# Block-sparse attention with a two-layer network behind it: attention steps placed 0.08 units later in a hand-written order, from the fourth chunk on

## The chip, the cores and the metric

The kernel runs on one core of one Trainium2 chip. Five engines work side by side, each through its own list of instructions in order: TensorE (PE, with its weight loads PEld), VectorE (DVE), ScalarE (ACT), GpSimd (POOL) and SyncE (SP), which issues nearly all DMAs. They wait for one another through semaphores. The metric is device time in microseconds (us), a median over several runs.

## The reference

The kernel computes masked attention, and then a two-layer network over the attention's output. Cut to what matters:

```python
def _attn_ref(q, k, v, sampled_blocks):          # 4 batches, 8 heads, 768 positions, 64 wide
    scores = scale * np.matmul(q, k.transpose(0, 1, 3, 2))
    # a block of 32 queries sees: its neighbours, blocks 0 and 23, three sampled blocks;
    # the queries of blocks 0 and 23 see all keys
    scores = np.where(mask, scores, -1000000000.0)
    scores = scores - np.max(scores, axis=-1, keepdims=True)
    attn = np.exp(scores)
    attn = attn / (np.sum(attn, axis=-1, keepdims=True) + 1e-09)
    return np.matmul(attn, v)
def _moe_ref(x, w_in, w_out):                    # 3072 tokens, 512 wide, 2048 in the middle
    h = x @ w_in
    g = h - np.tanh(h)
    return g @ w_out
```

## The kernel before

The 3072 tokens go through the network in six chunks of 512, each made of four blocks of 32 queries of all four batches (`CHUNKS`). A chunk is worked off in 16 **units**, one for each 128 columns of the hidden layer, so that the program has 96 units. A unit u is:

- `first(u, c)`, c from 0 to 3: three products of 128x512 each, 12 in all, into the bank `hb[u % 2]` (bank 4 or 5 of PSUM). Weights and data are split into a high and a low part, which makes three products of one.
- `bent(u, ...)`: the function h - tanh(h), on ScalarE (`w`, `t`, `qq`, `mk`, `gh`), VectorE (`th`, `p1`, `p2`, `p3`, `cp`) and GpSimd (`gl`). `cp` is VectorE's predicated copy into the tile `t`; it is the last to read the bank of h.
- `second(u, j)`, j from 0 to 3: three products of 128x512 each (called a triple below), added into the banks 0 to 3. They run two units later than the unit's `first`.

When a chunk ends, `store` brings the four banks out, some two units later, on ScalarE and VectorE.

Attention is cut into **steps** (`Unit`, A0 to A55 below). A step of one block or of a part of an edge block is: `scores` (32 small products, 64 rows by 32 columns of the array, into the banks 6 and 7), `most` (VectorE, two maxima), `exps` (ScalarE, j = 1 and then j = 0), `turn` (8 transposes on TensorE, back into the banks 6 and 7), `copy` (one half on VectorE, one on ScalarE), `accum` (64 small products, 128 rows by 32 columns of the array) and `norm` (VectorE), then `put` on ScalarE and GpSimd into the operand of the chunk that comes next. For the two edge blocks three steps make one result, and `weigh` and `join` bring them together on VectorE. `accum` writes its result into bank 4 or 5, which is also a bank of h: it waits for the `cp` that last read this bank, and the next `first` into it waits for `norm`.

The order on every engine is the order of the program, and that is written by hand: every piece of work is put into a list with a due time in units (`at(time, f, ...)`), the list is sorted by time, and the engines run their instructions in that order. The attention that makes chunk m runs beside the network of an earlier one, in steps at the due times of `SLOTS`:

```python
SLOTS = [[0.17, 1, 2, 3, 4, 5], [22 + i for i in range(8)]] + [[16 * m + i * 16 // 11 for i in range(11)] for m in range(2, 5)]
    self.t = dict(s=t(0), m=t(0.08), e1=t(0.2), e0=t(0.3), turn=t(turn), c0=t(turn + 0.06), c1=t(turn + 0.05), pv=t(prod), norm=t(prod + 0.1))
```

The steps of chunks 3 to 5 (the fourth chunk on) are A24 to A55, in units 32 to 78. `scores` of a step is due 0.55 into its unit, and `accum` of the step before it 0.52 into the same unit. Where the next step lies one unit on, `turn` is due 0.66 after `scores` (`QUICK`); where it lies two units on, 1.0 after it (`TURN`). The network's own due times stay as they are: `second(u, j)` at u + 2.5 + 0.125 j, so that in every unit the four triples are due at 0.5, 0.625, 0.75 and 0.875; `first(u, c)` at u + 0.125 c; `p3` at u + 1.27 and `cp` at u + 1.49. The `join` pieces of the first two edge blocks are put where `quiet` finds the largest distance from due times of attention.

All instructions show as line L78 in the profile, since one helper issues them; they are told apart by engine, operation and tile.

Of the kernel before, what the change touches and what calls it, by code (L numbers as in the profile page):

```python
# [32 lines left out]
NU = NTOK // P // CT * NFT  # L33

LEAD, T0, RATE = 10, 10.25, 0.62
QUICK, TURN = 0.66, 1.0
NQ = 4
KEPT = 3
VW = H * (D + 1) // 2
# [27 lines left out]
class InOrder:  # L67


    class Engine:  # L70
        def __init__(self, tc, engine):
            self.tc, self.engine = tc, engine
# [44 lines left out]
class Unit:  # L117
# [27 lines left out]
    def at(self, half, j):  # L145

        return (half, self.b) if self.b else (self.f, (NB - 1) * half)


class Attention:  # L150
    def __init__(self, tc, k, q, v, samp, rows, ffn, ident, banks, att, sm, f2, rv, at):
        self.tc, self.nc = tc, InOrder(tc)
        self.k, self.q, self.v, self.ffn, self.ident, self.banks = k, q, v, ffn, ident, banks
        self.sm, self.f2, self.att, self.rv = sm, f2, att, rv
        self.ks = att.tile([P, 2, H, S], F32, name="ks")
        self.vws, self.krs, self.loans = {}, {}, {}
        ffn.lent = self.lent
        self.kx, self.vx = (att.tile([1, 66], I32, name=f"{n}x") for n in "kv")
        self.held = {}
        self.vals, self.qs, self.ve = {}, {}, {}  # L160
        self.ms, self.nbs, self.ps, self.pts, self.nbe, self.es, self.wts = ({} for _ in range(7))
        self.kept = [ffn.spare.bitcast(F32)[:, 256 * i : 256 * i + 256] for i in range(3)]

        units = []
        last = {}

        def add(c, time, **kw):
            u = Unit(len(units), c, time, **kw)
            u.i, u.before = c, last.get(c)
            if u.n < LEAD - 2:  # L170
                u.i, u.before = u.n % 2, units[u.n - 2] if u.n > 1 else None
            elif u.n < LEAD:
                u.before = units[u.n - 2]
            if u.b:
                last[c] = u
            units.append(u)

        for c in range(2):
            for b in CHUNKS[0]:
                add(c, 0, b=b)  # L180
        for c in range(2):
            add(c, 0, b=CHUNKS[1][0])
        for m, blocks in list(enumerate(CHUNKS))[1:]:
            steps = [(c, dict(b=b)) for b in blocks if 0 < b < NB - 1 for c in range(2)]
            edges = [(g // 2, dict(f=g % 2, k=k)) for g in EDGES.get(m, ()) for k in range(3)]
            steps += edges
            for i, (c, kw) in enumerate(steps[2 * (m == 1) :]):
                slots = SLOTS[m - 1]
                following = slots[i + 1] if i + 1 < len(slots) else 16 * m if m > 2 else slots[i] + 1
                add(c, slots[i] + 0.55, prod=following + 0.52, **kw)  # L190
        lead = lambda x: (x - T0) * RATE
        for u in units[:2]:
            at(lead(-9.05), self.load_q, u)
        for bt in range(2):
            at(lead(-9), self.load_k, 0, bt)
        at(lead(-9.1), self.load_samples, samp, rows)
        for bt in range(2):
            at(lead(-8.9), self.load_k, 1, bt)
        for u in units:
            t, n = u.t, u.n  # L200
            if u.b:
                if n > 1:
                    at(max(t["s"] - 2.0, units[n - NQ].t["s"] + 0.01) if n >= NQ else lead(-8.95 + 0.01 * n), self.load_q, u)
                at(max(t["s"] - 1.2, u.before.t["s"] + 0.01 if u.before else lead(-3)), self.gather_k, u)
                at(max(t["s"] - 2.0, u.before.t["pv"] + 0.01) if u.before else lead(-3 + 0.1 * n), self.gather_v, u)
            else:
                if u.k == 0:
                    at(units[n - 1].t["s"] + 0.02, self.load_q, u)
                at(units[n - 2].t["pv"] + 0.02, self.load_ve, u)
            at(t["s"], self.scores, u)  # L210
            at(t["m"], self.most, u)
            at(t["e1"], self.exps, u, 1)
            at(t["e0"], self.exps, u, 0)
            at(t["turn"], self.turn, u)
            at(t["c1"], self.copy, u, 1)
            at(t["c0"], self.copy, u, 0)
            at(t["pv"], self.accum, u)
            at(t["norm"], self.norm, u)
            if u.b:
                for x in "hl":  # L220
                    at(t["norm"] + (0.1 if x == "h" else 0.15), self.put, u, x)
            elif u.k == 2:
                at(t["e0"] + 0.12, self.weigh, u)
                end = 2 * u.c + u.f in EDGES[len(CHUNKS) - 1]
                quiet = iter([t["norm"] + 0.1 + 0.08 * j for j in range(6)] if end else self.quiet(units[u.n + 1 :], t["norm"]))
                for k in range(3):
                    for s in range(1 + k):
                        at(next(quiet), self.join, u, k, s)
                for i in range(2):
                    for x in "hl":  # L230
                        at(t["norm"] + 0.65 + 0.2 * i if end else LATE + 0.5 * (2 * u.c + u.f) + 0.25 * i, self.put, u, x, i)
# [489 lines left out]
```

## Time and profile before

| | before |
|---|---|
| time, median of 3 runs | 786.54 us (785.02 to 787.48) |
| the profiled execution's own time | 785.86 us |
| its span, first to last instruction | 784.1 us |
| TensorE busy | 728.9 us, 93% of the span |
| VectorE busy | 549.9 us, 70% |
| ScalarE busy | 479.2 us, 61% |
| GpSimd busy | 337.2 us, 43% |
| TensorE's mean granted clock over the span | 0.98 |

Shares of busy time are means over stages with different limits. The first 330 us or so hold the conversion of the weights and the attention of the first three chunks; the change touches what runs after about 312 us of the span, and up to about 675 us. Names in the rows: `ps` is any bank of PSUM, `kr` and `ks` are gathered and whole keys, `vw` and `ve` values, `pt` the transposed exponentials, `wo` and `wro` the second layer's weights, `t` the tile that `cp` completes. A product whose second operand is `gh` or `gl` is of `second`, one from `x` of `first`, one from `q` of `scores`, one from `pt` of `accum`, one from `ident` of `turn`.

### The profile page before, as it was taken

How to read it: one execution, taken by the hardware profiler on the slowest of the kernel's cores; microseconds unless marked ns; L12 is line 12 of the kernel's file. 1: busy time of each engine (PE TensorE's matmuls, PEld its weight loads, DVE VectorE, ACT ScalarE, POOL GpSimd, SP SyncE). 2: the span in 40 equal slices, each digit the busy share in tenths (PEclk: the TensorE clock that was granted, in tenths of full speed). 3: DMA queues.
4: the chain of work that ended last, by engine and by line, in shares of the span. 5: the costliest groups of instructions: out<-in, count | busy, mean ns of one | idle time of the engine just before them, and what ended most of it. 6: DMA issues, size and time to landing. Idle time of an engine off the chain costs nothing.

```text
span 784.1 us, 20699 instructions
## 1 busy us (share of the span) xinstructions
PE 728.9 (93%) x8128; PEld 564.7 (72%) x8128; DVE 549.9 (70%) x970; ACT 479.2 (61%) x1021; POOL 337.2 (43%) x406
## 2 busy tenths in 40 slices
PE   1777887999999999999999999999999998999996
PEld 0555555878777777777777777777877776788884
DVE  4566777779875765777676678676777675875653
ACT  1576756577767766565665666665666555554553
POOL 3685764667687646244322434321432211221211
PEclk9899999999999999999999999999999999999998
DMA  8887674489685686275746166565157364246542
GB/s 347 268 268 239 201 224 161 164 320 363 228 262 171 193 275 205 79 233 175 280 149 205 37 200 230 185 228 184 69 158 265 127 217 163 82 135 219 187 158 80
DMA packets 54260, 155.49 MB, mean 198 GB/s; under 512 B 9107, under 2 KB 15764, under 8 KB 53652
## 3 DMA queue, kind: packets, MB, share of 16 engines
q1 hardware_dynamic: 53780, 153.65, 58.6%
q8 instruction: 64, 1.05, 0.5%
q10 hardware_dynamic: 384, 0.52, 0.2%
q14 instruction: 32, 0.26, 0.1%
HBM read 133.17 MB, written 20.97 MB: 197 GB/s over the span
## 4 chain that ended last, share of the span: by engine, by line
PE 71%; DVE 7%; ACT 3%; issue 2%; POOL 1%; DMA 0%; DVEq 0%; POOLq 0%
PE ps L78 71%; DVE ps L78 3%; DVE t L78 1%; POOL gl L78 1%; DVE m L78 0%; ACT p L78 0%; ACT t L78 0%; DVE e L78 0%; ACT hs L78 0%; ACT wo L78 0%; ACT u L78 0%; DVE ob L78 0%; DVE cvti L78 0%; DVE cvto L78 0%; ACT gh L78 0%
## 5 line engine op out<-in xcount | busy, mean ns | idle before, releaser
L78 PE MATMUL ps<-x,wi 128*128 128x512 f32 x888 | 221.2, 393 | 0.0
L78 POOL TENSOR_TENSOR gl<-t,gh 128x512 fp32r<-128x512 f32 x96 | 124.3, 1295 | 215.3 <-ACT gh L78 69.5
L78 PE MATMUL ps<-wo,gh 128*128 128x512 f32 x592 | 192.2, 407 | 0.0
L78 PEld LDWEIGHTS ps<-x,wi 128*128 128x128 f32 x888 | 164.9, 188 | 35.5
L78 PEld LDWEIGHTS ps<-wo,gh 128*128 128x128 f32 x592 | 108.6, 190 | 36.9 <-issue 15.0
L78 ACT ACTIVATE u<-ps 128x512 f32<-128x512 f32 x96 | 57.3, 597 | 108.2 <-PE ps L78 108.2
L78 PE MATMUL ps<-wo,gl 128*128 128x512 f32 x296 | 117.6, 399 | 0.7 <-POOL gl L78 0.7
L78 POOL TENSOR_TENSOR x<-xt,x 128x256 fp32r<-128x256 f32 (+1 forms) x48 | 34.3, 715 | 161.8 <-ACT x L78 158.3
L78 POOL COPY kr<-ks 128x256 f32 (+2 forms) x188 | 98.5, 617 | 11.9 <-DMA ks<-k 11.7
L78 DVE TENSOR_REDUCE m<-ps 128x2 f32<-128x512 f32 x112 | 70.9, 673 | 19.1 <-PE ps L78 17.2
L78 DVE COPY_PREDICATED t<-mk,ps 128x512 f32<-128x512 int32 x96 | 71.8, 748 | 10.1 <-DVE ps L78 0.9
L78 DVE TENSOR_TENSOR ps<-ps,u 128x512 f32<-128x512 f32 x96 | 66.5, 692 | 13.7 <-ACT t L78 13.7
L78 ACT ACTIVATE p<-ps,nb 128x256 f32<-128x256 f32 x176 | 73.8, 471 | 2.9
L78 DVE SCALAR_TENSOR_TENSOR ps<-qq,ps 128x512 f32<-128x512 f32 x96 | 66.4, 692 | 12.9 <-ACT qq L78 8.6
L78 PEld LDWEIGHTS ps<-vw,pt 128*32 128x32 f32 x2816 | 44.4, 113 | 38.6 <-DVE t L78 10.1
L78 PE MATMUL ps<-vw,pt 128*32 128x65 f32 x2816 | 52.5, 227 | 20.4 <-DMA vw<-v 9.3
L78 ACT ACTIVATE qq<-u,bias 128x512 f32<-128x512 f32 x96 | 69.3, 722 | 0.0
L78 ACT ACTIVATE mk<-u,bias 128x512 f32<-128x512 f32 x96 | 69.1, 720 | 0.0
L78 DVE SCALAR_TENSOR_TENSOR ps<-u,ps 128x512 f32<-128x512 f32 x96 | 66.6, 693 | 2.5
L78 DVE TENSOR_TENSOR t<-t,ps 128x512 f32<-128x512 f32 x64 | 43.5, 680 | 35.2 <-ACT t L78 35.1
L78 PE MATMUL ps<-ident,p 128*128 128x128 f32 x448 | 62.4, 283 | 5.6 <-ACT p L78 4.2
L78 PEld LDWEIGHTS ps<-wo,gl 128*128 128x128 f32 x296 | 56.1, 189 | 15.4 <-POOL gl L78 1.9
(98 smaller groups left out, 980.2 us busy)
## 6 DMA issues: line engine op xcount, KB each, us to landing
wi<-w2i SPq DMA_DIRECT2D x65, 512.0 KB, 4.7
wo<-w2o SPq DMA_DIRECT2D x65, 512.0 KB, 3.7
vw<-v SPq DMA_DIRECT2D x186, 130.0 KB, 2.9
q<-q SPq DMA_DIRECT2D x52, 128.0 KB, 4.3
ve<-v SPq DMA_DIRECT2D x24, 260.0 KB, 4.0
ks<-k SPq DMA_DIRECT2D x4, 1536.0 KB, 8.4
rawo<-w SPq DMA_DIRECT2D x12, 512.0 KB, 4.3
rawi<-w SPq DMA_DIRECT2D x10, 512.0 KB, 4.7
```

The source lines that it names most:

```text
L78: r = f(*args, **kw)
```

## The change

One number is added, `SHIFT` = 0.08, to both due times of every step of chunks 3 to 5; all other times of a step are counted from these two.

```diff
-QUICK, TURN = 0.66, 1.0
+QUICK, TURN, SHIFT = 0.66, 1.0, 0.08
...
-                add(c, slots[i] + 0.55, prod=following + 0.52, **kw)
+                add(c, slots[i] + 0.55 + SHIFT * (m > 2), prod=following + 0.52 + SHIFT * (m > 2), **kw)
```

No instruction is added or taken away; the rows of each engine change places. Three places show how.

TensorE, unit 39: the end of `second(37, 0)` (bank `ps0`), `accum` of A28 (64 products into `ps4`, of which the first four and the last four are shown), `scores` of A29 (32 products into `ps6` and `ps7`) and `second(37, 1)` (bank `ps1`). Before:

```order
L78 MATMUL ps0_72<-wo37_5030,gh_37_5080 128x512 x2
L78 MATMUL ps0_72<-wo37_5030,gl_37_5089 128x512
L78 MATMUL ps4_76<-vw00_16_2920,pt28_1_5068 32x65 x4
...
L78 MATMUL ps4_76<-vw01_16_2921,pt28_0_5070 32x65 x4
L78 MATMUL ps6_78<-kr1_17_3090,q29_15_4982 32x256
...
L78 MATMUL ps7_79<-kr1_17_3090,q29_15_4982 32x256
L78 MATMUL ps1_73<-wo37_5030,gh_37_5080 128x512 x2
L78 MATMUL ps1_73<-wo37_5030,gl_37_5089 128x512
```

Now:

```order
L78 MATMUL ps0_72<-wo37_5030,gh_37_5080 128x512 x2
L78 MATMUL ps0_72<-wo37_5030,gl_37_5089 128x512
L78 MATMUL ps4_76<-vw00_16_2920,pt28_1_5073 32x65 x4
...
L78 MATMUL ps4_76<-vw01_16_2921,pt28_0_5075 32x65 x4
L78 MATMUL ps1_73<-wo37_5030,gh_37_5080 128x512 x2
L78 MATMUL ps1_73<-wo37_5030,gl_37_5089 128x512
L78 MATMUL ps6_78<-kr1_17_3090,q29_15_4987 32x256
...
L78 MATMUL ps7_79<-kr1_17_3090,q29_15_4987 32x256
L78 MATMUL ps2_74<-wo37_5030,gh_37_5080 128x512 x2
```

The triple for bank `ps1` now stands between `accum` and `scores`. This is so in all 31 places where an `accum` was followed at once by a `scores` (A24 with A25 up to A54 with A55). `turn` moves by one triple as well, from after 6 products of `first` to after 9 (18 steps), or from after one triple of `second` to after two (14 steps). `accum` stays behind the first triple of `second`.

VectorE, the same step, from `most` of A29 on: `th`, `p1`, `p2` of unit 39, the copy of `pt29_1`, `p3` (from `qq_39`) and `cp`. Before:

```order
L78 TENSOR_REDUCE m29_5185<-ps7_79 128x2
L78 TENSOR_REDUCE m29_5185<-ps6_78 128x2
L78 TENSOR_TENSOR t_39_5173<-t_39_5173,ps5_77 128x512
L78 TENSOR_TENSOR ps5_77<-ps5_77,u_39_5119 128x512
L78 SCALAR_TENSOR_TENSOR ps5_77<-u_39_5119,ps5_77 128x512
L78 COPY pt29_1_5235<-ps7_79 128x512
L78 SCALAR_TENSOR_TENSOR ps5_77<-qq_39_5206,ps5_77 128x512
L78 COPY_PREDICATED t_39_5173<-mk_39_5213,ps5_77 128x512
```

Now:

```order
L78 TENSOR_REDUCE m29_5185<-ps7_79 128x2
L78 TENSOR_REDUCE m29_5185<-ps6_78 128x2
L78 TENSOR_TENSOR t_39_5157<-t_39_5157,ps5_77 128x512
L78 TENSOR_TENSOR ps5_77<-ps5_77,u_39_5119 128x512
L78 SCALAR_TENSOR_TENSOR ps5_77<-u_39_5119,ps5_77 128x512
L78 SCALAR_TENSOR_TENSOR ps5_77<-qq_39_5202,ps5_77 128x512
L78 COPY pt29_1_5236<-ps7_79 128x512
L78 COPY_PREDICATED t_39_5157<-mk_39_5213,ps5_77 128x512
```

`p3` now stands ahead of the copy of the transposed tile.

VectorE, unit 49, in which the store of chunk 2 lies: `cp` of unit 48, `norm` of A35 (its first and its last row), `most` of A36, a `join` piece of an edge block (`e32`), a `store` (`ob2_1`) and `th` of unit 49. Before:

```order
L78 COPY_PREDICATED t_48_6142<-mk_48_6175,ps4_76 128x512
L78 TENSOR_SCALAR rs35_6270<-ps4_76 128x4
...
L78 STREAM_TRANSPOSE xt35_6269<-x35_6273 128x256
L78 TENSOR_REDUCE m36_6279<-ps7_79 128x2
L78 TENSOR_REDUCE m36_6279<-ps6_78 128x2
L78 TENSOR_TENSOR e32_5792<-e32_5792,w34_5970 128x260
L78 TENSOR_SCALAR ob2_1_6299<-ps1_73 128x512
L78 TENSOR_TENSOR t_49_6267<-t_49_6267,ps5_77 128x512
```

Now:

```order
L78 COPY_PREDICATED t_48_6124<-mk_48_6175,ps4_76 128x512
L78 TENSOR_TENSOR e32_5795<-e32_5795,w34_5977 128x260
L78 TENSOR_SCALAR rs35_6280<-ps4_76 128x4
...
L78 STREAM_TRANSPOSE xt35_6279<-x35_6283 128x256
L78 TENSOR_REDUCE m36_6286<-ps7_79 128x2
L78 TENSOR_REDUCE m36_6286<-ps6_78 128x2
L78 TENSOR_SCALAR ob2_1_6292<-ps1_73 128x512
L78 TENSOR_TENSOR t_49_6252<-t_49_6252,ps5_77 128x512
```

The `join` piece has moved ahead of `norm`. The same holds in unit 65; in unit 33, where chunk 0 is stored, it is the first of four store instructions (`sums0` from `ps0`) that moves ahead of `norm`. On ScalarE, `gh` of the unit before moves ahead of both `exps`, and `qq` goes in between them. On GpSimd and SyncE the pieces keep their order among those that wait for one another; loads of `q` and gathers of `v` stand a few rows later.

## Rows read from the trace of the kernel before

**Rows 1.** The profile page: its first line.

```profile
span 784.1 us, 20699 instructions
```

**Rows 2.** Engines in four stretches: start:end, length, busy time by engine, granted clock, DMA.

```profile
core 0: us, PE busy (x) PEld busy (x) DVE busy (x) ACT busy (x) POOL busy (x), PEclk, DMA share, GB/s
340.00:440.00 100.00, 100.00 (x1244) 77.99 (x1243) 69.78 (x121) 60.61 (x132) 32.74 (x43) 1.00 0.55 189
460.00:560.00 100.00, 100.00 (x1162) 78.42 (x1160) 72.59 (x128) 61.80 (x132) 35.14 (x48) 1.00 0.60 203
580.00:640.00 60.00, 60.00 (x720) 47.02 (x712) 44.20 (x77) 37.49 (x83) 16.26 (x19) 1.00 0.58 202
650.24:653.65 3.41, 3.41 (x36) 2.02 (x21) 2.08 (x4) 0.97 (x4) 0.00 (x0) 0.50 0.61 152
```

**Rows 3.** TensorE's waits from 318 to 700 us: total, times, longest.

```profile
PE ps L78 <- DVE t L78: 4.2, 4, 2.2
```

**Rows 4.** TensorE's timeline: an `accum` alone among triples, then a `scores` alone.

```profile
300.71 1.11 PE L78 MATMUL ps<-vw,pt 128*32 128x65 f32 x64
301.76 0.73 PE L78 MATMUL ps<-wo,gh 128*128 128x512 f32 x2
...
302.56 0.63 PE L78 MATMUL ps<-wo,gh 128*128 128x512 f32 x2
...
303.26 0.63 PE L78 MATMUL ps<-wo,gh 128*128 128x512 f32 x2
...
312.25 0.63 PE L78 MATMUL ps<-wo,gh 128*128 128x512 f32 x2
...
313.04 1.09 PE L78 MATMUL ps<-kr,q 64*32 64x256 f32 x32
314.06 0.73 PE L78 MATMUL ps<-wo,gh 128*128 128x512 f32 x2
...
314.87 0.63 PE L78 MATMUL ps<-wo,gh 128*128 128x512 f32 x2
```

**Rows 5.** TensorE's timeline: one `QUICK` step, `accum` to `accum`.

```profile
367.79 1.11 PE L78 MATMUL ps<-vw,pt 128*32 128x65 f32 x64
368.83 1.09 PE L78 MATMUL ps<-kr,q 64*32 64x256 f32 x32
...
373.43 1.03 PE L78 MATMUL ps<-ident,p 128*128 128x128 f32 x8
...
376.47 1.11 PE L78 MATMUL ps<-vw,pt 128*32 128x65 f32 x64
```

**Rows 6.** VectorE's timeline in the same step.

```profile
370.21 1.25 DVE L78 TENSOR_REDUCE m<-ps 128x2 f32<-128x512 f32 x2
...
372.70 0.70 DVE L78 SCALAR_TENSOR_TENSOR ps<-u,ps 128x512 f32<-128x512 f32 x1
374.14 0.69 DVE L78 COPY pt<-ps 128x512 f32<-128x512 f32 x1 [0.74 <-ACT qq L78]
374.75 0.69 DVE L78 SCALAR_TENSOR_TENSOR ps<-qq,ps 128x512 f32<-128x512 f32 x1
375.53 0.75 DVE L78 COPY_PREDICATED t<-mk,ps 128x512 f32<-128x512 int32 x1
```

**Rows 7.** Timeline of all engines around the edge steps A52 and A53.

```profile
638.00 1.11 PE L78 MATMUL ps<-ve,pt 128*32 128x65 f32 x64
639.04 1.09 PE L78 MATMUL ps<-ks,q 64*32 64x256 f32 x32
...
640.25 1.29 DVE L78 TENSOR_REDUCE m<-ps 128x2 f32<-128x512 f32 x2 [0.64 <-PE ps L78]
...
648.98 1.11 PE L78 MATMUL ps<-ve,pt 128*32 128x65 f32 x64 [2.22 <-DVE t L78]
```

**Rows 8.** VectorE's timeline where a chunk is stored: unit 33, then unit 49.

```profile
324.28 1.27 DVE L78 SCALAR_TENSOR_TENSOR sums<-ps,sums 128x512 f32<-128x512 f32 x2
...
448.77 0.45 DVE L78 TENSOR_TENSOR e<-e,w 128x260 f32<-128x260 f32 x1
449.14 0.68 DVE L78 TENSOR_SCALAR ob<-ps 128x512 f32<-128x512 f32 x1
```

## The prediction, made before the changed kernel had run

> **What bounds the kernel now.** I read the stretches first, because the change touches only units 32 to 78. In the three steady stretches of that stage TensorE is busy for the whole of 100, 100 and 60 us at the full granted clock, while VectorE, the next busiest, has some 70 of 100 [rows 2]. The reader is to see that there is nothing to win there by waiting less: TensorE's list sets the time, and only its length, or a wait that comes in anew, can change it. Next I read TensorE's waits over the whole stage: 4.2 us in four waits, all for VectorE's tile `t`, that is for `cp`, and the longest is 2.2 us [rows 3]. All four stand ahead of an `accum`, three where a chunk is stored and one where an edge block is joined [rows 7]. Behind the longest, the granted clock stands at 0.50, the lower of its two levels (1.2 of 2.4 GHz), for 3.41 us [rows 2], which at half speed costs about 1.7 us. So the most that any rearrangement could win here is 4.2 + 1.7 = 5.9 us.
>
> **The change part by part.**
>
> *The triple between `accum` and `scores`.* Triples among themselves start 0.70 us apart (302.56 to 303.26) [rows 4]. The first triple behind an `accum` takes 0.80 (301.76 to 302.56), the first behind a `scores` 0.81 (314.06 to 314.87), and the last one ahead of a `scores` 0.79 (312.25 to 313.04) [rows 4]. So a change from small to full tiles costs some 0.10 on the far side and one from full to small 0.09 on the near side. Does the change from `accum` to `scores`, which goes away, give something back? `accum` takes 1.04 with a `scores` behind it (367.79 to 368.83) [rows 5] and 1.05 with a triple behind it (300.71 to 301.76) [rows 4]: nothing comes back. No row of before shows a triple with an `accum` ahead and a `scores` behind. The lower bound is 0, if such a triple hid both; the upper is the sum, 0.10 + 0.09 = 0.19, and I take the upper, since its two ends are the same changes of tile that the rows show one by one. There are 31 such places. In 27 of them nothing else changes: 27 x 0.19 = 5.1 us.
>
> *`turn` one triple later.* It is moved past a triple of full tiles, with full tiles on both sides as before: no cost in itself. What shrinks is the time from `turn` to `accum`, in which both copies and `cp` must be done. In a `QUICK` step it is 3.04 us now (373.43 to 376.47) [rows 5], and about 2.34 then. Whether VectorE keeps up I count from the start of an `accum`. `scores` starts 1.04 + 0.70 + 0.19 = 1.93 after it; `most` starts 1.21 after `scores` when VectorE is idle (639.04 to 640.25) [rows 7], so at 3.14 instead of 2.42 (370.21 - 367.79) [rows 5, 6]. `p2` follows 2.49 later (372.70 - 370.21) [rows 6], at 5.63, and `p3`, now ahead of the copy, ends near 7.0. `turn` starts at 5.64 + 0.19 + 0.70 = 6.53; the copy starts 0.71 later [rows 5, 6], at 7.24, `cp` 0.61 behind it (the distance from 374.14 to 374.75) [rows 6], at 7.85, and it ends at 8.60. `accum` is due at 8.68 + 0.19 = 8.87. The slack is 0.27 us, against 0.19 before (376.28 to 376.47). So I cost it at nothing: it is hidden by the `p3` that ran behind the copy and now runs ahead of it, in the time in which VectorE had waited for `turn` (0.74 us of idle time) [rows 6]. The steps with `TURN` have a whole further unit. On ScalarE `qq` takes the place of `gh` between the two `exps`, an activation of the same width. Without this cover each of the 13 `QUICK` steps that are left when the special ones below are taken out would wait.
>
> *The four special places.* There VectorE runs without a pause from `most` to `cp`, and TensorE waits for it; a later `most` is a later `accum`. At the joined edge block `most` starts 2.25 after `accum` (638.00 to 640.25) [rows 7] and would start at 3.14: 0.89 us. Where chunks 2 and 3 are stored, 3.14 - 2.42 = 0.72 comes in, and the `join` piece, 0.37 of the chain (448.77 to 449.14) [rows 8], moves to the time in which VectorE waits for `accum`: 0.35 each. Where chunk 0 is stored, one of two equal store instructions (1.27 for the pair [rows 8], so about 0.63) moves out of the chain in the same way: about 0.1. Together 0.89 + 2 x 0.35 + 0.1 = 1.7 us, with the triple's price in it already. The clock's loss I leave as it is: the wait ahead of it only gets longer.
>
> *Queues.* SyncE's and GpSimd's pieces for a step move with it, past work that doesn't wait for them; in the steady stretches TensorE waits for no DMA [rows 3], and `accum`, which frees the buffers, keeps its place.
>
> **The sum.** 5.1 + 1.7 = 6.8 us on a span of 784.1 [rows 1], so about 790.9 of span, or 785.86 + 6.8 = 792.7 for this execution. The median of the runs lies 0.7 above it, at 786.54; against that I forecast 793.3 us, 0.9% slower. What a measurement here can tell from no change is about 0.3%, 2.4 us. The forecast's own range is 791.5 to 795.
>
> One page speaks for a smaller price. The Trainium skill (TensorEngine Tiling (Array Packing), Key Properties) says that a change of the tiling mode drains TensorE. `accum` and `scores` are of different modes, so that by this rule there was a drain between them as well, and the split adds one drain a step and not two. The trace agrees that a change costs some 0.1 us; that `accum` takes 1.04 or 1.05 whichever follows fits with the rule too.
>
> **The rivals.**
>
> 1. *Only one end of the triple is paid.* If the pass from `accum` to `scores` holds a drain that the two rows above cannot tell from running work, or if the weights for `scores` are loaded under the triple, the price is about 0.10 a step: 27 x 0.10 = 2.7, with 1.7 for the special places 4.4, or 790.9 us. Against it: triples next to small tiles pay at either end by themselves [rows 4].
> 2. *VectorE falls behind in the `QUICK` steps.* The slack of 0.27 us is small beside a path of 8.9, and `mk`, which `cp` needs, now stands behind both `exps` and `qq`. Were `cp` late by 0.3 in each of the 13, 3.9 us would be added: 797.2. For it speaks how close the count is; against it, that the slack comes out no smaller than before.
> 3. *The triple hides both changes of tile.* Then only the special places are left: 786.54 + 1.7 = 788.2, no change that can be told.
> 4. *Faster: VectorE's list, sorted anew, ends the four waits for `cp`.* `p3`, a store and the `join` pieces move into idle time; if that lets `cp` be done before each of the four `accum`, 5.9 us go (the waits and the slow stretch behind the longest). It decides only where the split costs less than (5.9 - 2.4) / 31 = 0.11 us a step: with no price for the split the time is 780.6, with the whole price 786.54 + 31 x 0.19 - 5.9 = 786.5. Against it: `most` comes later at all four, and each of them has VectorE as its chain [rows 7].
>
> **How the numbers follow.** I give the forecast 0.66, rival 1 0.10, rival 2 0.12, rival 3 0.07 and rival 4 0.05. Slower by over 0.3% are the forecast and rivals 1 and 2: 0.88. Within it are rival 3 and a little of rival 4: 0.08. Faster is the rest of rival 4: 0.04. The range, 789.8 to 797.3, reaches from rival 1 to rival 2 and leaves out rivals 3 and 4.
>
> **What would show it.** In the trace after, in the steady stretches: TensorE still without idle time, a triple of about 0.89 us between `accum` and `scores`, `accum` to `accum` in a `QUICK` step at 8.87 instead of 8.68, and `p3` ahead of the copy. TensorE's waits for `t` should still be four, at about 5 us in total, the longest near 3 us with the lower clock behind it. A triple of 0.70 or 0.80 would make rival 3 or 1 right; more than four waits for `t`, rival 2; fewer, rival 4. The prediction would also be wrong if a longer wait brought the clock down for longer, or at a second place.

## The result, and the profile after

The changed kernel takes 793.43 us (median of 6 runs, 789.78 to 795.09), the kernel before 786.70 us beside it (6 runs). The ratio is 1.0096, with a 95% interval of 1.0075 to 1.0117: 1.0% slower, where 0.9% was forecast.

The profiled execution has a span of 791.7 us, 7.6 more than before [rows 1]. Where it went is read from two starts in TensorE's timeline, the last `accum` ahead of the change (A23) and the last one in it (A55). Before:

```profile
300.71 1.11 PE L78 MATMUL ps<-vw,pt 128*32 128x65 f32 x64
...
673.52 1.11 PE L78 MATMUL ps<-ve,pt 128*32 128x65 f32 x64
```

After:

```profile
301.11 1.11 PE L78 MATMUL ps<-vw,pt 128*32 128x65 f32 x64
...
680.79 1.11 PE L78 MATMUL ps<-ve,pt 128*32 128x65 f32 x64
```

From A23 to A55 it was 372.81 us and is 379.68: 6.9 of the 7.6 us lie in the part that was changed; 0.4 were there before it began, and 0.3 come behind it.

TensorE still works without a pause in the steady stretches. The same stretches as in [rows 2] after the change:

```profile
340.00:440.00 100.00, 100.00 (x1214) 76.32 (x1212) 68.00 (x118) 61.08 (x130) 32.52 (x43) 1.00 0.57 191
460.00:560.00 100.00, 100.00 (x1167) 76.22 (x1152) 70.65 (x127) 61.74 (x134) 33.41 (x44) 1.00 0.62 204
580.00:640.00 60.00, 59.60 (x711) 45.29 (x710) 43.39 (x80) 37.67 (x86) 14.84 (x18) 1.00 0.60 200
```

The stretch from 580 us now holds the wait where chunk 3 is stored. TensorE's waits from 318 to 710 us, which answer to [rows 3], are the same four:

```profile
PE ps L78 <- DVE t L78: 4.2, 4, 2.3
```

So the kernel is not slower because TensorE waits more. Its list takes longer. TensorE's timeline of the step of [rows 5] (A28 to A29) after the change:

```profile
368.93 1.11 PE L78 MATMUL ps<-vw,pt 128*32 128x65 f32 x64
369.98 0.73 PE L78 MATMUL ps<-wo,gh 128*128 128x512 f32 x2
370.55 0.40 PE L78 MATMUL ps<-wo,gl 128*128 128x512 f32 x1
370.87 1.09 PE L78 MATMUL ps<-kr,q 64*32 64x256 f32 x32
371.90 0.73 PE L78 MATMUL ps<-wo,gh 128*128 128x512 f32 x2
...
372.70 0.63 PE L78 MATMUL ps<-wo,gh 128*128 128x512 f32 x2
...
375.47 1.03 PE L78 MATMUL ps<-ident,p 128*128 128x128 f32 x8
```

The reader is to see the triple between `accum` and `scores`: from 369.98 to 370.87 it takes 0.89 us, where a triple among triples takes 0.70 [rows 4]; the first triple behind `scores` still takes 0.80, and `accum` (1.05) and `scores` (1.03) take what they took before to 0.01. VectorE in the same step, as in [rows 6]:

```profile
372.08 1.29 DVE L78 TENSOR_REDUCE m<-ps 128x2 f32<-128x512 f32 x2 [0.65 <-PE ps L78]
...
374.60 0.70 DVE L78 SCALAR_TENSOR_TENSOR ps<-u,ps 128x512 f32<-128x512 f32 x1
375.40 0.70 DVE L78 SCALAR_TENSOR_TENSOR ps<-qq,ps 128x512 f32<-128x512 f32 x1
376.11 0.69 DVE L78 COPY pt<-ps 128x512 f32<-128x512 f32 x1
376.72 0.74 DVE L78 COPY_PREDICATED t<-mk,ps 128x512 f32<-128x512 int32 x1
```

`most` starts 3.15 us after `accum` and `cp` ends 8.53 after it, 0.37 ahead of the next `accum` at 377.83.

The times from one `accum` to the next, worked out from the starts in the timelines of all kernels of this study, are used in the rest of the text:

| accum to accum, us | before | after | shift_011 | accum_halves | p3_behind | split_only | spread |
|---|---|---|---|---|---|---|---|
| QUICK, typical | 8.69 | 8.90 | 8.70 | 9.03 | 9.42 | 9.08 | 8.70 |
| TURN, typical | 14.21 | 14.44 | 14.24 | 14.57 | 14.43 | 14.54 | 14.24 |
| store of chunk 0 (A24 to A25) | 9.94 | 10.10 | 9.34 | 10.38 | 10.11 | 10.70 | 8.77 |
| store of chunk 2 (A35 to A36) | 9.13 | 9.52 | 8.97 | 9.80 | 9.52 | 9.85 | 8.97 |
| store of chunk 3 (A46 to A47) | 9.13 | 9.51 | 8.98 | 9.79 | 9.52 | 9.85 | 8.98 |
| joined edge block (A52 to A53) | 10.98 | 11.26 | 10.50 | 11.54 | 11.48 | 11.67 | 8.71 |
| the TURN step behind it (A53 to A54) | 15.81 | 15.94 | 14.22 | 16.07 | 15.96 | 14.54 | 14.24 |

The last row holds the slow stretch behind the wait of the joined edge block: from 656.4 to 659.8 us of the changed kernel's trace the granted clock stands at 0.50, as it did before [rows 2]. In the traces of shift_011, split_only and spread it stays at 1.00 there, and the step is 1.4 to 1.7 us shorter than in the change.

### The profile page after: what moved, and what is told of

It is laid out like the page before. It is cut to its first block, busy times and chain, and to the rows that moved or that the text cites. A ratio compares the mean times of both kernels' runs of the same rounds, so it can differ in the third digit from the quotient of the medians.

```text
span 791.7 us, 20680 instructions
## 1 busy us (share of the span) xinstructions
PE 732.7 (93%) x8128; PEld 560.3 (71%) x8128; DVE 547.4 (69%) x970; ACT 481.1 (61%) x1021; POOL 337.2 (43%) x406
## 3 DMA queue, kind: packets, MB, share of 16 engines
q8 instruction: 64, 1.05, 0.5%
## 4 chain that ended last, share of the span: by engine, by line
PE 70%; DVE 7%; ACT 4%; issue 2%; POOL 1%; DMA 0%; SPq 0%; DVEq 0%; POOLq 0%
PE ps L78 70%; DVE ps L78 4%; DVE t L78 1%; POOL gl L78 1%; DVE m L78 1%; ACT wo L78 0%; ACT p L78 0%; ACT hs L78 0%; DVE ob L78 0%; ACT t L78 0%; ACT u L78 0%; DVE cvti L78 0%; ACT qq L78 0%; DMA vw<-v 0%; DVE cvto L78 0%
## 5 line engine op out<-in xcount | busy, mean ns | idle before, releaser
L78 PEld LDWEIGHTS ps<-wo,gh 128*128 128x128 f32 x592 | 105.5, 188 | 37.4 <-issue 14.6
L78 PE MATMUL ps<-kr,q 64*32 64x256 f32 x1408 | 51.3, 399 | 16.2 <-POOL kr L78 15.7
```

What stands on the lines that cost most here:

```text
L78: r = f(*args, **kw)
```

## The experiments

**shift_011: attention as late or later, without the split.**

```diff
-QUICK, TURN, SHIFT = 0.66, 1.0, 0.08
+QUICK, TURN, SHIFT = 0.66, 1.0, 0.11
```

> The same edit with 0.11 in place of 0.08: accum and scores are then both behind the second triple and stand side by side again, while everything else of the step is as late as in the change or later. Theory (the price is the extra pass between small and full tiles in each step): the 27 ordinary places lose their 0.21 to 0.23 us, which is 5.9 us, and what p3, the join pieces and the store won by moving ahead is kept: about 785 us, TensorE's QUICK cycle from accum to accum back at 8.69 to 8.71. Rival (attention that comes later costs by itself, by VectorE or by the chain of exps, and not by the split): 793 us or more, with waits of TensorE for t in the steady stretch.

Measured: 784.38 us (12 runs) beside 786.06 for the kernel before; ratio 0.9987 (0.9966 to 1.0008). TensorE's timeline of the same step shows the pair side by side again, and both behind two triples:

```profile
367.04 1.11 PE L78 MATMUL ps<-vw,pt 128*32 128x65 f32 x64
368.08 1.09 PE L78 MATMUL ps<-kr,q 64*32 64x256 f32 x32
369.11 0.73 PE L78 MATMUL ps<-wo,gh 128*128 128x512 f32 x2
...
372.68 1.03 PE L78 MATMUL ps<-ident,p 128*128 128x128 f32 x8
...
375.74 1.11 PE L78 MATMUL ps<-vw,pt 128*32 128x65 f32 x64
```

A step is 8.70 us again, as the theory had it, though attention comes even later in the unit than in the change. The rival falls: lateness by itself costs nothing. But `accum` has moved behind the second triple too, so the time from `turn` to `accum` is 3.06 us, as it was before (3.04); the shorter one of the change (2.36) is tested in p3_behind and split_only. TensorE's waits from 318 to 720 us:

```profile
PE ps L78 <- DVE t L78: 2.3, 2, 1.7
```

The two waits for `cp` where chunks 2 and 3 are stored are gone, since the `join` pieces and `p3` keep the places that the change gave them and `most` follows `accum` after 2.42 us again. A part of the time won against the kernel before, 1.6 us, is the slow stretch that is missing (the last row of the table).

**accum_halves: the triple inside `accum`.**

```diff
-QUICK, TURN, SHIFT = 0.66, 1.0, 0.08
+QUICK, TURN, SHIFT = 0.66, 1.0, 0.11
...
-            at(t["pv"], self.accum, u)
+            if u.n >= 24:
+                at(t["pv"] - 0.03, self.accum, u, (1,))
+                at(t["pv"], self.accum, u, (0,))
```

> Shift 0.11, but accum of steps A24 to A55 cut in its two halves (j = 1 and j = 0), one ahead of the second triple and one behind it; scores stands beside the second half. Nothing lies between accum and scores, but a triple lies between small tiles, once a step. Theory (a triple between small tiles costs 0.2 us wherever it stands): 32 times 0.2 us over shift_011, so the QUICK cycle at about 8.9 and, with the later maxima at the four special places, about 793 to 795 us. Rival (the price belongs to the place between accum and scores, such as the later scores): the time of shift_011.

Measured: 797.69 us, ratio 1.0141 (1.0093 to 1.0188). The rival falls, and the theory's price is too low: the step has 9.03 us, 0.33 over shift_011 and not 0.20. TensorE's timeline, a triple between the halves and `scores` behind the second half:

```profile
371.28 0.66 PE L78 MATMUL ps<-vw,pt 128*32 128x65 f32 x32
371.87 0.73 PE L78 MATMUL ps<-wo,gh 128*128 128x512 f32 x2
...
372.77 0.66 PE L78 MATMUL ps<-vw,pt 128*32 128x65 f32 x32
373.36 1.09 PE L78 MATMUL ps<-kr,q 64*32 64x256 f32 x32
```

The triple takes 0.90, as in the change. But each half of `accum` takes 0.59, together 1.18, where the whole takes 1.04: if a run's time is a fixed share and an equal one for each product, the fixed share is about 0.14 us (an estimate from these two lengths), and it is there with a triple behind the run (the first half) as with `scores` behind it (the second). So a whole further run costs 0.20 + 0.14 = 0.34, against the 0.33 by which the step grew. In the change `accum` and `scores` were two runs before and are two runs after, and only the triple's two ends are paid.

**late_gh: one `gl` put back beside the `join` pieces.**

```diff
-                    at(u + t, self.bent, u, y)
+                    at(u + (1.85 if (u, y) == (73, "gh") else t), self.bent, u, y)
```

> The change, with one piece moved back: gh of unit 73 stands behind the first half of exps of A53, as before the change, so that GpSimd's gl of that unit starts after the maxima and runs beside the join additions. Theory (the join chain of A52 got 0.6 us shorter than I had counted because gl no longer runs beside the addition of two e tiles, which took 0.95 us before and 0.43 after): an addition near 0.95 again, the cycle from accum A52 to accum A53 at about 11.8 instead of 11.26. Rival (p3 ahead of the copy made it shorter): 11.26, additions of 0.43.

Measured, one run with a profile: from accum A52 to accum A53 it is 12.14 us (wait 2.99) against 11.26 in the change; the time was 794.99. All other steps are as in the change. TensorE's wait, GpSimd's timeline and then VectorE's in that step:

```profile
657.63 1.40 PE L78 MATMUL ps<-ve,pt 128*32 128x65 f32 x64 [2.99 <-DVE t L78]
```

```profile
651.09 1.29 POOL L78 TENSOR_TENSOR gl<-t,gh 128x512 fp32r<-128x512 f32 x1 [7.80 <-ACT gh L78]
```

```profile
649.84 0.42 DVE L78 TENSOR_TENSOR e<-e,w 128x260 f32<-128x260 f32 x1
...
651.37 1.29 DVE L78 TENSOR_TENSOR e<-e,w 128x260 f32<-128x260 f32 x1
652.70 0.43 DVE L78 TENSOR_TENSOR e<-e,e 128x260 f32<-128x260 f32 x1
```

The multiplication that starts 0.28 us after `gl` ends 0.28 us after it: 1.29 us instead of 0.42, which is 0.87 of the 0.88 us by which the step grew. This is another piece than the one that was expected to be long, but the mechanism is the theory's, and the rival (the order of `p3` and the copy) falls for this part. The kernel before had the same meeting, with the addition. Its timeline:

```profile
642.70 1.29 POOL L78 TENSOR_TENSOR gl<-t,gh 128x512 fp32r<-128x512 f32 x1 [7.11 <-ACT nbe L78]
...
643.33 0.95 DVE L78 TENSOR_TENSOR e<-e,e 128x260 f32<-128x260 f32 x1
```

In the change `gl` is over long before the additions:

```profile
645.83 1.29 POOL L78 TENSOR_TENSOR gl<-t,gh 128x512 fp32r<-128x512 f32 x1 [3.34 <-issue]
...
651.02 0.43 DVE L78 TENSOR_TENSOR e<-e,e 128x260 f32<-128x260 f32 x1
```

The Trainium skill (SBUF — State Buffer, SBUF: two separate sides) says that a GpSimd operation that reads SBUF and a VectorE operation with two inputs from SBUF take the same pair of ports, that the one that starts first keeps it for its whole instruction, and that the other waits. The trace agrees in the main: a VectorE operation of 0.42 us takes 1.29 and ends 0.28 behind `gl`, so that all but some 0.14 of its own time lies behind it.

**p3_behind: the cover taken away.**

```diff
-                    at(u + t, self.bent, u, y)
+                    at(u + (1.355 if u >= 32 and y == "p3" else t), self.bent, u, y)
```

> The change, with p3 of units from 32 on put back behind the copy of the transposed tile. Theory (p3 ahead of the copy is what hides the shorter way from turn to accum): cp ends about 9.4 us after accum in a QUICK step, where accum is due at 8.90, so TensorE waits about 0.5 us in each of the 14 ordinary QUICK steps and 0.2 more at each of the four special places: about 801 us. Rival (there is slack enough without it): 793.4, no new waits.

Measured: 800.97 us, ratio 1.0194 (1.0151 to 1.0237), as the theory had it. TensorE's waits from 318 to 720 us:

```profile
PE ps L78 <- DVE t L78: 10.7, 18, 2.5
```

The 18 are the four special places and 14 QUICK steps, as expected. A typical one waits about 0.45 us and takes 9.42, 0.52 more than in the change. VectorE's timeline of one of them:

```profile
379.01 0.69 DVE L78 SCALAR_TENSOR_TENSOR ps<-u,ps 128x512 f32<-128x512 f32 x1
380.58 0.69 DVE L78 COPY pt<-ps 128x512 f32<-128x512 f32 x1 [0.88 <-PE ps L78]
381.19 0.69 DVE L78 SCALAR_TENSOR_TENSOR ps<-qq,ps 128x512 f32<-128x512 f32 x1
381.98 0.73 DVE L78 COPY_PREDICATED t<-mk,ps 128x512 f32<-128x512 int32 x1
```

VectorE waits 0.88 us for `turn` with `p3` behind it. The expected 0.2 more at each special place came at the joined edge block alone; where a chunk is stored, the cycle is as in the change.

**split_only: TensorE's new list, with the old places of nearly all else beside it.**

```diff
-                    at(u + LAG + 0.5 + 0.125 * j + 0.5 * i, self.second, u, j, part)
+                    at(u + LAG + 0.5 + (0.035 if j == 1 and u >= 30 and not end else 0.125 * j) + 0.5 * i, self.second, u, j, part)
...
-            turn = min(QUICK, prod - time - 0.27) if prod < time + 1 else TURN
+            turn = min(QUICK + 0.08 * (time > 32), prod - time - 0.27 + 0.08 * (time > 32)) if prod < time + 1 else TURN
```

(made from the kernel before; ScalarE and GpSimd keep their old lists, and on VectorE one thing moves that the expectation doesn't name: the copy comes later with `turn`, so that `p3` stands ahead of it in 18 steps, as in the change)

> The kernel before, with TensorE's list put in exactly the order of the change (the second triple due 0.535 into its unit, turn 0.08 later in the QUICK steps), while norm, most, exps, gh, qq, the join pieces and the store keep their places of before. Theory (TensorE's order makes the price; the new places on VectorE and ScalarE only take some of it back at the four special places): QUICK cycle 8.90 as in the change; the special cycles longer than in the change, by 0.4 to 0.5 each where chunks 2 and 3 are stored, 0.6 where chunk 0 is stored and 0.5 or more at the joined edge block: about 795.5 us. Rival (the places on VectorE and ScalarE make the price): near 787 us.

Measured: 799.28 us, ratio 1.0189 (1.0155 to 1.0223). The rival falls, and the expectation is missed by 3.8 us: the ordinary steps are slower than in the change too, 9.08 and 14.54. The special ones are longer than in the change by 0.60 (chunk 0), 0.33 and 0.34 (chunks 2 and 3) and 0.41 (the edge block), the last three a little less than expected. ScalarE's and VectorE's rows of a QUICK step, between its two `accum`:

```profile
370.76 1.13 PE L78 MATMUL ps<-vw,pt 128*32 128x65 f32 x64
...
377.09 0.72 ACT L78 ACTIVATE qq<-u,bias 128x512 f32<-128x512 f32 x1
377.70 0.72 ACT L78 ACTIVATE mk<-u,bias 128x512 f32<-128x512 f32 x1
377.84 0.70 DVE L78 SCALAR_TENSOR_TENSOR ps<-qq,ps 128x512 f32<-128x512 f32 x1 [0.71 <-ACT qq L78]
378.38 0.60 ACT L78 ACTIVATE pt<-ps 128x512 f32<-128x512 f32 x1
378.45 0.68 DVE L78 COPY pt<-ps 128x512 f32<-128x512 f32 x1
379.05 0.75 DVE L78 COPY_PREDICATED t<-mk,ps 128x512 f32<-128x512 int32 x1
...
379.85 1.12 PE L78 MATMUL ps<-vw,pt 128*32 128x65 f32 x64
```

`p3` waits 0.71 us for `qq`, which here stands behind both `exps`, so that the copy is late and `cp` ends at 379.80, and `accum` comes at 379.85 instead of 379.66 (370.76 + 8.90), where a step of 8.90 would have put it. So `qq` between the two `exps` is a part of the cover as well. In the TURN steps `accum` comes just behind `cp` too. Rows of the TURN step that ends with the `accum` at 370.76:

```profile
365.90 0.60 ACT L78 ACTIVATE pt<-ps 128x512 f32<-128x512 f32 x1 [1.53 <-PE ps L78]
366.39 0.59 ACT L78 ACTIVATE t<-ps 128x512 f32<-128x512 f32 x1
...
367.02 0.69 DVE L78 TENSOR_TENSOR t<-t,ps 128x512 f32<-128x512 f32 x1 [0.86 <-ACT t L78]
...
369.95 0.75 DVE L78 COPY_PREDICATED t<-mk,ps 128x512 f32<-128x512 int32 x1
```

ScalarE's copy waits 1.53 us for `turn`, `t` of the next unit stands behind it, and VectorE's `th` waits for `t`; `cp` ends at 370.70, 0.06 ahead of `accum`. In the change `t` stands ahead of this copy, and in the same step `cp` ends 0.89 us ahead of `accum`. That this order makes the 0.1 is read from the rows; no run changed it alone.

**spread: two of the special places eased.** From shift_011:

```diff
-                quiet = iter([t["norm"] + 0.1 + 0.08 * j for j in range(6)] if end else self.quiet(units[u.n + 1 :], t["norm"]))
+                spread = [75.56, 75.57, 76.56, 76.57, 77.56, 77.57]
+                quiet = iter(spread if u.n == 52 else [t["norm"] + 0.1 + 0.08 * j for j in range(6)] if end else self.quiet(units[u.n + 1 :], t["norm"]))
...
-                    at(u + LAG + 0.64 + 0.125 * j + 0.5 * end, *to)
+                    at(u + LAG + 0.64 + (0.01 if ENDS.index(u + 1) == 3 and j == 1 else 0.125 * j) + 0.5 * end, *to)
```

The `put` pieces of A52 move to 78.2 and 78.4, and the tiles `e` of A53 to A55 lie in the buffer of `kr0`, which no step needs any more.

> shift_011 with two of the four special places eased: the six join pieces of A52 go two by two into the idle time ahead of norm in units 75 to 77 instead of all into unit 74 (the tiles of A53 to A55 lie in a dead buffer, so that they don't wait for it), and the second store of chunk 0 goes ahead of norm. Theory: the waits left in shift_011 (1.73 and 0.57 us) go, so about 782 us, 0.5% under the kernel before. Rival (another wait takes their place, such as the operand of the last chunk, which comes later): 784.4.

Measured: 782.35 us (12 runs) beside 785.19 for the kernel before; ratio 0.9970 (0.9953 to 0.9987). The view of TensorE's waits is empty from unit 32 to 78, and from A52 to A53 it is 8.71 us. Where chunks 2 and 3 are stored, 0.27 us over a QUICK step are left (8.97 and 8.98), as in shift_011. They lie inside `turn`, whose second half waits for `exps`, as TensorE's weight loads show:

```profile
451.80 0.42 PEld L78 LDWEIGHTS ps<-ident,p 128*128 128x128 f32 x4 [0.29 <-ACT p L78]
```

It has the lowest median of this study; the 782 us that were expected came, but only 0.3% under the kernel before, which ran at 785.19 beside it. The times alone don't tell it from shift_011 (0.9987, with an interval that overlaps); the traces do, by the special places.

## Why the prediction was right, and where its sizes were off

**The triple between `accum` and `scores`: right, a little too small.** The triple costs the sum of its two ends, 0.89 to 0.90 us instead of 0.70. Each ordinary cycle grew by 0.21 (QUICK) or 0.23 (TURN), not by 0.19; in a QUICK step 0.02 of it lies in the products of `first` that `turn` now cuts nine to three (3.64 us with `turn` in the step shown, 3.62 before), which the prediction had at nothing. The 27 ordinary places together gave 5.7 us (the 6.9 less the 1.2 of the next point), where 5.1 was forecast. The rows of the step add up to it, and the runs bear it out: with the pair side by side again (shift_011) the step is 8.70, and with TensorE's list of the change beside mostly old lists (split_only) it is no shorter than in the change.

**The four special places: right in kind, too large by 0.5 us.** The store of chunk 0 cost 0.16 (0.1 forecast), those of chunks 2 and 3 0.39 and 0.38 (0.35), the joined edge block 0.28, where the term said 0.89. There `most` did come 3.14 us after `accum`, as counted; but from `most` to `cp` the chain got 0.6 us shorter. `gh`, which I had only noted as standing ahead of `exps`, runs while VectorE waits for `scores`, GpSimd's `gl` follows it, and it is over before the `join` pieces begin. So the addition that had met `gl` takes 0.43 again and not 0.95, which is 0.5 of the 0.6. late_gh lets them meet again, and 0.88 us come back. For the same reason TensorE's four waits stayed at 4.2 us, where I had looked for 5, with 2.3 as the longest and not 3. The two errors of size had opposite signs, 0.6 too low and 0.5 too high, so that the sum of 6.8 met 6.9 better than its terms did.

**`turn` one triple later, costed at nothing: right but for the 0.02 above, and for the reason given.** The slack was counted at 0.27 us and is 0.37. `p3` ahead of the copy is the cover: without it (p3_behind) a QUICK step waits 0.45 us. The prediction put VectorE's idle 0.74 us down to `turn`, while the row names `qq` [rows 6]; that the copy follows `turn` is borne out by p3_behind, where it starts 0.70 us after `turn` (0.71 before) and the row names TensorE's bank. What I had passed over is ScalarE's share of the cover. I took `qq` between the `exps` for an exchange of equals; split_only shows that with `gh` there instead, `p3` is late even ahead of the copy. The new places on ScalarE and of the `join` and store pieces on VectorE together hold back some 5 to 7 us: 799.28 against 793.43, but 14.1 against 6.7 over the kernel before beside each, and 5.1 from A23 to A55 of the two traces. `p3` is not in this, since split_only has it ahead as well.

**Rival 1 falls.** Its sum rested on one drain of 0.10 a step. As for the rule of the Trainium skill (TensorEngine Tiling (Array Packing), Key Properties) that a change of tiling mode drains TensorE, accum_halves fits with it: half an `accum` takes the same 0.59 us ahead of `scores` as ahead of a triple. Whether a drain makes its fixed time, no run shows. But the further change costs what the triple has at its two ends, 0.19 to 0.20, and not one drain of 0.10. Nor are the weights for `scores` loaded under the triple; their load starts with the first product of `scores`:

```profile
370.87 0.61 PEld L78 LDWEIGHTS ps<-kr,q 64*32 64x32 f32 x32 [0.36 <-issue]
```

**Rival 2** did not happen; p3_behind and split_only show that it hangs on the order of two lists. **Rival 3** falls with the triple of 0.89. **Rival 4** is half true: in shift_011 the new order on VectorE does end two of the four waits, and in the change it could not, since the split makes `most` 0.7 us later.

## What to carry to other kernels

Where a full engine sets the time, the price of a new order is in its seams: count how often the list changes between kinds of instruction, and read each change's price as the difference of the same block with and without that neighbour. A shift of a few hundredths in a list sorted by due times moves pieces past each other or doesn't; what matters is what it passes, so 0.08 cost 1.0% and 0.11 nothing that can be told from noise. A move that is free on the full engine can still rest on a cover in two other engines' lists, and the cover is best shown by taking it away.

## What the runs showed of the hardware that was not expected

A VectorE operation with both inputs in SBUF, 0.42 us alone, took 1.29 when GpSimd's `gl` had started 0.28 us ahead of it. A run of 32 `accum` products took 0.59 us and one of 64 took 1.04, which gives about 0.14 us of fixed time for a run (an estimate), whether `scores` or a triple came behind it. And the fall of the granted clock did not follow the length of TensorE's wait alone: behind the wait of 2.2 us before, the 2.3 after, the 2.5 in p3_behind and the 2.99 in late_gh it stood at the lower of its two levels (1.2 of 2.4 GHz) for 3.4 us, but not behind the wait of 1.73 in shift_011 or that of 2.70 in split_only, whose stretch behind the wait (in the columns of [rows 2]) is:

```profile
662.44:667.44 5.00, 5.00 (x108) 3.61 (x109) 2.29 (x5) 1.24 (x5) 0.00 (x0) 1.00 0.42 118
```

Each of these is one trace of its kernel; what decides it stays open.
